# Attention and gated FFN on one core: first norm split in two, and one half of a batch's transposes issued among the output tiles

## The chip, the cores and the metric

The kernel runs on one core of a Trainium2 chip. The metric is device time in microseconds (us), the median of several executions. The engines of the core are named as in the profile: PE is TensorE's matmul, PEld its weight load, DVE is VectorE, ACT is ScalarE, POOL is GpSimd and SP is SyncE. SP, POOL and ACT also issue the DMAs. The code gives each engine its own list of instructions, in the order in which it issues them; an instruction carries the semaphore waits that it needs.

## The reference

```python
batch, n_heads, seq, head_dim = (8, 12, 448, 64)      # q, k, v: float32
n_tokens, d_model, d_ff = (3584, 768, 1536)

scores = scale * np.matmul(q, k.transpose(0, 1, 3, 2))
attn = np.maximum(scores, 0.0) ** 2 / S
x = np.matmul(attn, v)            # then [batch, seq, heads*head_dim] -> [3584, 768]

rms = np.sqrt(np.mean(x * x, axis=-1, keepdims=True) + 1e-06)
xn = x / rms * rms_g
g = xn @ w_gate
silu = g * (1.0 / (1.0 + np.exp(-g)))
val = xn @ w_val
return silu * val @ w_out
```

There are eight batches of 448 tokens. Each goes through an attention without softmax (a squared ReLU of the scores), an RMS norm over 768 features, and a gated FFN of width 1536.

## The kernel before

The order of the work is written out by hand. Matmuls of one batch's FFN (the `main` list) are interleaved by `weave` (L17) with steps of the next batch's attention (the `sides` list, each with the place in `main` before which it is issued). All operands of matmuls are bf16.

**Transposing q and k.** Scores need q and k with the head dimension on partitions. For batches 0 and 1, `pe_transposes(b, j)` (L128) does one pair of heads `j` on PE: 16 small matmuls against an identity into one PSUM tile `psT` (k in one half, q in the other), and one copy of 128x896 to the SBUF tile `qkT`, by DVE for batch 0 and by ACT for batch 1. For batches 2 and up, DMA does it: `transposes(b, half)` (L150) issues two DMA transposes on SP, `qT` (L157) and `kT` (L161), for six heads each, and `fill(b, half, gpsimd)` (L167) issues two SBUF copies on POOL (L169, L170) which bring a second copy of the transposed q to the other 64 partitions. `trans_fill` (L622) does both. `fetch(b)` (L88) loads q, k and v of a batch by three DMAs on POOL.

**Scores and values.** `pair_scores` (L194, batch 1) and `head_scores` (L213, batches 2 and up) do two matmuls into a PSUM tile `psS` (tag "psS", two buffers), then ReLU to the SBUF tile `r`, on ACT or, for some of them, on DVE. `squares` (L244) squares on DVE. `attend` (L255) multiplies with v into `psAV`, and `leave` (L279) takes it out of PSUM: `xT` (scaled by the norm's gain), and `x2`, the square for the norm, both on ACT. For batch 0's last pair `leave` squares on ACT and writes `xT` and both halves of `xD` on DVE (L294). `swap` (L302) issues two DMAs on SP which write `xD`, that is `xT` with its two halves of partitions exchanged. Matmuls of the FFN take their weight rows of one head on 64 partitions, so that gate and value run side by side on two halves of the array: six rounds use `xT` ("own", r = 0 to 5), and six use `xD` (r = 6 to 11). Two such matmuls side by side are called a pair here.

**The norm.** `norm_stat` (L401) sums `x2` by 12 matmuls with ones into `psSS`, takes the root on ACT (with a table load, and another for Silu after it), the reciprocal on DVE (`rhalf`, L424), and spreads it to `rstd` over all partitions by two copies on DVE and two on ACT (L431, L433). `norm_apply` (L436) multiplies `xT` and `xD` by `rstd` on DVE (L445), six instructions each. For batch 0 the products go to new tiles. From batch 1 on they are written over `xT`, so the product of a row must wait until the swap has read that row. For batches 2 and up the swap follows the norm.

**The stretch from batch 0's attention to its FFN** (L652 to L680). So that PE has work while batch 0's norm is not ready, three blocks of the FFN (`early_block`, PSUM tiles `psE` from a pool "mm" of four buffers) run on the raw `xT` and `xD` (`part(fb, r, ...)` does rounds r of block fb), and are scaled by `rstd` later (`early_out` copies them to SBUF on ACT, `early_scale`, `early_rest`). `units[tail:]` are the last five steps of batch 0's attention: the squares of the last pair, `leave` and `swap` of pair 4, `attend` and `leave` of pair 5. `steps` are the steps of batch 1's attention.

**The stretch from batch 0's FFN to batch 1's.** After `gate_value(0)`, six units of output tiles of batch 0 run (`out_tiles(0, 0, full)`, matmuls `psO` L399, copies `ost` L531 on ACT, stores L544 on SP). `steps[-1]`, the values, `leave` and `swap` of batch 1's last two pairs, is issued ahead of them, and `norm_stat(1)` and `norm_apply(1)` follow the first unit. Both `trans_fill(2, 0)` and `trans_fill(2, 1)` are sides of `gate_value(0)`, at 28 and 32. Then `gate_value(1)` begins, with batch 2's scores as sides: head h of batch 2 takes its `qT` and `kT` from half h // 6. Its other sides are `fetch(3)` at unit 2 and `trans_fill(3, 0)` at unit 13.

SP's order in this stretch is therefore: swaps of batch 1's pairs 0 to 3, four transposes of batch 2, the swap of batch 1's pairs 4 and 5, six stores, transposes of batch 3. POOL's is: `fetch(2)`, four fills, `fetch(3)`.

Of the kernel before, what the change touches and what calls it, by code (L numbers as in the profile page):

```python
# [8 lines left out]
FP32 = mybir.dt.float32  # L9
BF16 = mybir.dt.bfloat16  # L10
# [6 lines left out]
def weave(main, sides):  # L17

    sides = sorted(sides, key=lambda x: x[0])
    k = 0  # L20
    for n, f in enumerate(main):
        while k < len(sides) and sides[k][0] <= n:
            sides[k][1]()
            k += 1
        f()
    for _, f in sides[k:]:
        f()
# [7 lines left out]
def kernel(  # L35
# [11 lines left out]
    nc = tc.nc  # L47
    P = nc.NUM_PARTITIONS
# [79 lines left out]
    def pe_transposes(b, j):  # L128

        if b == 1 and j < 4:  # L130
            psT = ps_s.tile([P, 2, 1024], BF16, name="psT", tag="psS")
            psT = psT[:, 0, : 2 * S].rearrange("p (t s) -> p t s", t=2)
        else:
            psT = ps_m.tile([P, 2, S], BF16, name="psT", tag="mm")
        for ti, nm in enumerate(("k", "q")):
            for c in range(NCH):
                for hh in range(2):
                    nc.tensor.transpose(  # L138
                        out=psT[hh * D : (hh + 1) * D, ti, c * PC : (c + 1) * PC],
                        in_=ld[nm, b][:, 2 * j + hh, c * D : (c + 1) * D],  # L140
                        identity=ident[:],
                    )
        t = late["qkT"].tile([P, 2, S], BF16, name="qkT", tag="qkT")
        if b:
            nc.scalar.copy(out=t[:], in_=psT[:])
        else:
            nc.vector.tensor_copy(out=t[:], in_=psT[:])
        qkT[b, j] = t

# [44 lines left out]
    def pair_scores(b, j, c, on_dve):  # L194

        psS = ps_s.tile([P, 2, 512], FP32, name="psS", tag="psS")
        t = qkT[b, j]
        for hh in range(2):
            prt = slice(hh * D, (hh + 1) * D)
            flat = t[prt].rearrange("p t s -> p (t s)")  # L200
            nc.tensor.matmul(  # L201
                out=psS[:, hh, :S], lhsT=flat[:, c * PC : c * PC + P], rhs=t[prt, 1, :],
                start=True, stop=True,
            )
        if c % 2 == 0:
            raw[b, j, c] = apool.tile([PC, 2, 2, S], BF16, name="r", tag="r")
        r = raw[b, j, c - c % 2]
        if on_dve:
            nc.vector.tensor_relu(out=r[:, c % 2], in_=psS[:PC, :, :S])
        else:  # L210
            nc.scalar.activation(out=r[:, c % 2], in_=psS[:PC, :, :S], func=ACT.Relu)  # L211
# [126 lines left out]
    def attention_second(b):  # L338

        steps = []  # L340

        def visit(j, c):
            pair_scores(b, j, c, c == 3 and j > 0)
            if c == 0 and j:
                squares(b, j - 1, (2, 3))
            if c == 2:
                squares(b, j, (0, 1))

        def values(j):
            attend(b, (j, j + 1))  # L350
            leave(b, (j, j + 1))
            swap(b, j, j + 2)

        for j in range(HP):
            for c in range(NCH):
                steps.append(lambda j=j, c=c: visit(j, c))
                if c == 3 and j + 2 < HP:
                    steps.append(lambda j=j: pe_transposes(b, j + 2))
                if c == 3 and j in (2, 4):
                    steps.append(lambda j=j: values(j - 2))  # L360
                    steps.append(lambda: None)
        steps.append(lambda: squares(b, HP - 1, (2, 3)))
        steps.append(lambda: None)
        steps.append(lambda: values(HP - 2))
        return steps
# [24 lines left out]

    hTs, rstds = {}, {}

    def halves(ps, w, lhsT, rhs, start, stop):

# [4 lines left out]
    def norm_stat(b, psSS=None):  # L401


        if psSS is not None:
            psSS = psSS[:, :W]
        elif 1 < b < B - 1:
            psSS = ps_m.tile([P, S], FP32, name="psSS", tag="mm")[:, :W]
        else:
            psSS = ps_s.tile([P, 2, 512], FP32, name="psSS", tag="psS")[:, 0, :W]
        half = npool.tile([P, W], FP32, name="rhalf", tag="rhalf")  # L410
        rstd = npool.tile([P, S], FP32, name="rstd", tag="rstd")
        for kt in range(KT):
            for hf in (0, 1):
                prt = slice(HALF * hf, HALF * (hf + 1))
                nc.tensor.matmul(  # L415
                    out=psSS[prt, :], lhsT=ones_bf[:, prt],
                    rhs=x2s[b][:, kt, hf * W : (hf + 1) * W],
                    start=(kt == 0), stop=(kt == KT - 1),
                )
        nc.scalar.activation(  # L420
            out=half[:], in_=psSS, func=ACT.Sqrt, scale=1.0 / float(DM), bias=eps_col[:]
        )
        nc.scalar.activation(out=warm_act[:], in_=eps_col[:], func=ACT.Silu)
        nc.vector.reciprocal(out=half[:], in_=half[:])  # L424
        for own in (True, False):
            for hf in (0, 1):
                src = slice(HALF * hf, HALF * (hf + 1))
                dst = src if own else slice(HALF * (1 - hf), HALF * (2 - hf))
                o = rstd[dst, hf * W : (hf + 1) * W]
                if own:  # L430
                    nc.vector.tensor_copy(out=o, in_=half[src, :])  # L431
                else:
                    nc.scalar.copy(out=o, in_=half[src, :])  # L433
        rstds[b] = rstd
# [38 lines left out]
    def early_out(b, fb, parts):  # L473

        t = late["early"].tile([P, 2, S], FP32, name="gv", tag="gv")
        for part in range(2):
            nc.scalar.copy(out=t[:, part, :], in_=parts[part][:, :S])
        early[fb] = t
# [143 lines left out]
    def trans_fill(b, half):  # L622
        transposes(b, half)
        fill(b, half, nc.gpsimd)

    with tc.tile_pool(name="qkT", bufs=2, side="right") as tp, tc.tile_pool(
        name="early", bufs=EB, side="right"
    ) as ep:
        late["qkT"], late["early"] = tp, ep
        warm(12)  # L630
        steps = attention_second(1)

        def early_block(fb):
            return [ps_m.tile([P, S], FP32, name="psE", tag="mm")[:] for _ in range(2)]

        units = attention_first(0)
        tail = len(units) - 5
        for n, fn in enumerate(units[:tail]):
            fn()
            if n % 3 == 2:  # L640
                warm(2)


        raw_x = xTs[0], xDs[0]
        psSS = ps_m.tile([P, S], FP32, name="psSS", tag="mm")
        blocks = [early_block(0)]

        def part(fb, *rs):
            for r in rs:
                rounds(0, fb, blocks[fb], r, r + 1, raw_x)  # L650

        squares_last, leave_4, swap_4, attend_5, leave_5 = units[tail:]  # L652
        squares_last()
        part(0, *range(HP - 2))
        part(0, KT, KT + 1)
        leave_4()
        swap_4()
        attend_5()
        leave_5()
        part(0, KT + 2, HP - 2)  # L660
        pe_transposes(1, 0)
        norm_stat(0, psSS)
        blocks.append(early_block(1))
        part(0, HP - 1)
        part(1, *range(KT + 3))
        steps.pop(0)()
        part(0, KT + 3)
        pe_transposes(1, 1)
        steps.pop(0)()
        part(1, KT + 3)  # L670
        norm_apply(0)
        for fb in range(2):
            part(fb, KT + 4, KT + 5)
            early_out(0, fb, blocks[fb])
        for fb in range(2, EB):
            blocks.append(early_block(fb))
            for r0 in range(0, 2 * KT, KT):
                steps.pop(0)()
                rounds(0, fb, blocks[fb], r0, r0 + KT, raw_x)
            early_out(0, fb, blocks[fb])  # L680
        main = gate_value(0, EB, KT // 2)
        sides = along(6.4, 2, [lambda fb=fb: early_scale(0, fb) for fb in range(EB)])
        sides += along(10.4, 2, [lambda fb=fb: early_rest(0, fb) for fb in range(EB)])
        sides += along(0, (len(main) - 1) / len(steps), steps[:-1])
        sides += [(18.2, lambda: fetch(2))]
        sides += [(28, lambda: trans_fill(2, 0)), (32, lambda: trans_fill(2, 1))]
        weave(main, sides)
    late["ost"] = pool("ostage", 3)

# [2 lines left out]
    full = S // P  # L692
    ahead = []
    NB = 2 * FT
    weave(out_tiles(0, 0, full), [(0, steps[-1]), (1, lambda: norm_stat(1)), (1, lambda: norm_apply(1))])
    for b in range(1, B):
        main = gate_value(b)
        if b % 2:
# [46 lines left out]
```

## Time and profile before

| | us |
|---|---|
| median of 7 runs | 455.38 |
| the seven runs, sorted | 451.98, 452.86, 454.69, 455.38, 457.22, 457.36, 457.49 |
| the profiled execution | 457.35 |
| its span in the profile | 455.6 |
| PE busy | 441.6 (97%) |
| ACT busy | 285.1 (63%) |
| DVE busy | 265.0 (58%) |
| POOL busy | 53.6 (12%) |

The profiled execution took 1.75 us more than the span of its instructions. It lies at the upper end of the seven runs. All positions below are us from the start of the span. In the 20 us from 60 to 80, PE was busy for 20.00 and in those from 80 to 100 for 16.17, at a mean granted clock of 1.00 and 0.83. A PE matmul of 64x448 has a duration of 0.35 us at the full clock, and in a steady stream one pair follows another after 0.19 us. Ends of matmuls are modelled in the profile, so short gaps on PE can be missing from its list of waits.

### The profile page before, as it was taken

Reading aid. Unit: us, or ns where it says so; the run is one execution under the profiler, and the core shown is the slowest. Engines: PE = TensorE matmul, PEld = TensorE weight load, DVE = VectorE, ACT = ScalarE, POOL = GpSimd, SP = SyncE. Lnnn points to the kernel's source line nnn. Section 1 sums busy time; section 2 is a strip of 40 time slices with the busy share of each in tenths; the row PEclk is TensorE's granted clock in tenths of the full one; section 3 lists DMA queues with packets and bytes.
Section 4 is the critical chain, followed back from the end, with each engine's and each line's share of the span. In section 5 each row is a group of like instructions: output and inputs, shape, how many; then the busy total and the mean of one; then the engine's idle time right before and its main releaser. Section 6 shows DMA issues by size and latency. Waiting matters only on the chain.

```text
span 455.6 us, 10951 instructions
## 1 busy us (share of the span) xinstructions
PE 441.6 (97%) x4768; PEld 248.3 (55%) x4768; DVE 265.0 (58%) x341; ACT 285.1 (63%) x434; POOL 53.6 (12%) x79
## 2 busy tenths in 40 slices
PE   7998999889999999999999999999999999999996
PEld 3434555545556555655556555655556555565564
DVE  4979975368655566466754566476754366542210
ACT  4899886547766677566757577566757667552221
POOL 8343300400000300002000300003000000000000
PEclk9999999979999999999999999999999999999999
DMA  9999999995104995079913998069922900041013
GB/s 136 198 202 201 202 213 176 173 247 89 32 1 113 194 187 74 1 166 181 155 32 83 196 194 94 1 124 190 165 53 56 217 21 1 1 117 51 1 36 106
DMA packets 86832, 53.32 MB, mean 117 GB/s; under 512 B 36608, under 2 KB 80896, under 8 KB 86784
## 3 DMA queue, kind: packets, MB, share of 16 engines
q0 software_dynamic: 44496, 27.50, 42.1%
q1 hardware_dynamic: 41664, 24.56, 27.7%
q8 instruction: 37, 0.61, 0.6%
q10 hardware_dynamic: 624, 0.57, 0.4%
q14 instruction: 11, 0.09, 0.1%
HBM read 47.19 MB, written 11.01 MB: 128 GB/s over the span
## 4 chain that ended last, share of the span: by engine, by line
PE 91%; ACT 4%; DVE 2%; DMA 2%; issue 1%; ACTq 0%; SPq 0%; DVEq 0%
PE psG L465 39%; PE psO L399 22%; PE psAV L267 9%; PE psV L465 8%; PE psS L222 7%; PE psW L605 2%; DMA xD<-xT 2%; PE psS L181 1%; ACT r L191 1%; PE psT L138 1%; PE psS L201 1%; PE psE L465 1%; PE psSS L415 1%; DVE rhalf L424 1%; ACT ost L531 1%
## 5 line engine op out<-in xcount | busy, mean ns | idle before, releaser
L465 PEld LDWEIGHTS <-wgv_sb 64*128 64x128 bf16 x2304 | 122.3, 95 | 102.4 <-issue 16.7
L465 PE MATMUL psG<-xT,wgv_sb 64*128 64x448 bf16 x558 | 123.5, 352 | 3.8 <-DVE xT L445 3.8
L465 PE MATMUL psV<-xT,wgv_sb 64*128 64x448 bf16 x558 | 123.3, 353 | 0.0
L465 PE MATMUL psV<-xD,wgv_sb 64*128 64x448 bf16 x558 | 122.2, 351 | 0.0
L465 PE MATMUL psG<-xD,wgv_sb 64*128 64x448 bf16 x558 | 122.2, 351 | 0.0
L236 ACT ACTIVATE r<-psS 112x896 bf16<-112x896 f32 x108 | 96.1, 917 | 28.5 <-PE psS L222 28.4
L399 PE MATMUL psO<-wo_sb,hT 128*64 128x512 bf16 (+2 forms) x1368 | 113.7, 323 | 0.0
L511 DVE TENSOR_TENSOR hT<-sil,psV 128x448 bf16<-128x448 bf16 x93 | 57.6, 620 | 96.3 <-ACT sil L509 95.1
L399 PEld LDWEIGHTS <-hT 128*64 128x64 bf16 x1368 | 73.9, 110 | 36.1 <-issue 4.1
L509 ACT ACTIVATE sil<-psG 128x448 bf16<-128x448 f32 x93 | 50.7, 545 | 59.3 <-PE psV L465 41.9
L240 DVE TENSOR_TENSOR r<-r 112x1792 bf16<-112x1792 bf16 x72 | 78.4, 1089 | 11.1 <-ACT r L236 10.1
L531 ACT COPY ost<-psO 128x512 f32<-128x512 f32 (+2 forms) x57 | 26.2, 472 | 42.4 <-PE psO L399 35.8
L222 PE MATMUL psS<-qT,kT 64*128 64x448 bf16 (+1 forms) x288 | 47.4, 354 | 0.4 <-DVE r L234 0.4
L299 ACT ACTIVATE xT<-psAV,ga_sb 128x448 bf16<-128x448 f32 x47 | 27.5, 631 | 24.7 <-PE psAV L267 24.7
L234 DVE TENSOR_SCALAR r<-psS 112x896 bf16<-112x896 f32 x36 | 39.1, 1086 | 5.8 <-PE psS L222 5.8
L267 PE MATMUL psAV<-r,vb 112*64 112x448 bf16 x384 | 41.5, 356 | 0.0
L169 POOL DMA_DIRECT2D qT<-qT x12 | 6.5, 540 | 273.7 <-DMA qT<-qb 200.1
L424 DVE RECIPROCAL rhalf<-rhalf 128x224 f32<-128x224 f32 x8 | 12.4, 1554 | 38.0 <-ACT rhalf L420 38.0
L445 DVE TENSOR_TENSOR xT<-xT,rstd 128x448 bf16<-128x448 bf16 x48 | 26.5, 621 | 8.5 <-DMA xD<-xT 6.7
L267 PEld LDWEIGHTS <-vb 112*64 112x64 bf16 x384 | 19.4, 109 | 20.1 <-issue 8.7
L222 PEld LDWEIGHTS <-kT 64*128 64x128 bf16 (+1 forms) x288 | 16.9, 97 | 19.8 <-issue 8.7
L250 DVE TENSOR_TENSOR r<-r 112x1792 bf16<-112x1792 bf16 x23 | 24.5, 1086 | 1.8 <-ACT r L211 1.8
(57 smaller groups left out, 257.5 us busy)
## 6 DMA issues: line engine op xcount, KB each, us to landing
vb<-in_v_dram POOLq DMA_DIRECT2D x7, 672.0 KB, 18.5
qb<-in_q_dram POOLq DMA_DIRECT2D x6, 672.0 KB, 12.4
kb<-in_k_dram POOLq DMA_DIRECT2D x6, 672.0 KB, 15.3
qT<-qT POOLq DMA_DIRECT2D x24, 168.0 KB, 4.5
xD<-xT SPq DMA_DIRECT2D x24, 168.0 KB, 3.0
out_dram<-ost SPq DMA_DIRECT2D x7, 336.0 KB, 5.6
wgv_sb<-in_moe_w_gate_dram POOLq DMA_DIRECT2D x6, 384.0 KB, 16.8
wgv_sb<-in_moe_w_val_dram POOLq DMA_DIRECT2D x6, 384.0 KB, 16.9
```

Source lines behind the costliest of these rows:

```text
L222: nc.tensor.matmul(out=psS[: end - o, hf, :S], lhsT=flat[prt, o:end], rhs=qT[prt, 1 - hf : 3 - hf, h % HH], start=True, stop=True,)
L234: nc.vector.tensor_relu(out=r[:, cp], in_=src)
L236: nc.scalar.activation(out=r[:, cp], in_=src, func=ACT.Relu)
L240: nc.vector.tensor_tensor(out=r[:], in0=r[:], in1=r[:], op=ALU.mult)
L267: nc.tensor.matmul(out=part[hh * D : (hh + 1) * D, :], lhsT=ld["v", b][:, 2 * j + hh, c * D : (c + 1) * D], rhs=rsq[b, 2 * j + hh, c], sta ...
L299: nc.scalar.mul(out=xTs[b][:, j, :], in_=psAV[:, i, :], mul=ga_sb[:, j : j + 1])
L399: nc.tensor.matmul(out=ps[prt, :w], lhsT=lhsT[:, prt], rhs=rhs, start=start, stop=stop)
L445: nc.vector.tensor_tensor(out=x[:, kt, :], in0=raw_x[:, kt, :], in1=rstds[b][:], op=ALU.mult)
L465: nc.tensor.matmul(out=parts[part][:, :S], lhsT=wgv_sb[prt, h, fb * P : (fb + 1) * P], rhs=src[prt, kt, :], start=(r == 0), stop=(r == 2 * ...
L509: nc.scalar.activation(out=s[:], in_=psG, func=ACT.Silu)
L511: nc.vector.tensor_tensor(out=hT[:, fb, o : o + S], in0=s[:], in1=psV, op=ALU.mult)
L531: nc.scalar.copy(out=osts[i, t][:, o : o + w], in_=ps[:, :w])
```

## The change

1. `pe_transposes`: for batch 0's first pair, `psT` is two PSUM tiles instead of one, and each is copied on its own (two DVE copies of 128x448 in place of one of 128x896), the k half while q is still to come. For batch 1's first pair the copy moves from ACT to DVE.
2. `attention_second`: the ReLU of pair 1's last chunk moves from DVE to ACT (the fourth chunk of a pair is on DVE from pair 2 on, not from pair 1).
3. `norm_stat` ends after the reciprocal. The spread to `rstd` is a function of its own, `norm_spread`, called at once for all batches but 0. For batch 0, one visit of batch 1's scores (matmuls, and a ReLU on ACT) is written between the two.
4. The order of the parts after batch 0's attention is new: two own rounds of block 0 and batch 1's first transposes come ahead of `leave_4`, `swap_4`, `attend_5`, and more rounds come behind. Batch 1's second transposes move behind the first `early_out`.
5. `trans_fill(2, 1)` moves from `gate_value(0)` (side at 32) to the output tiles (side at 2). SP's order becomes: two transposes of batch 2, the swap of batch 1's pairs 4 and 5, the two stores of tile 0, the two other transposes of batch 2, four stores. POOL's order stays.

The number of instructions of each engine stays but for one more copy on DVE and what moves between DVE and ACT by 1 and 2.

```diff
+            parts = [psT[:, 0], psT[:, 1]]
+        elif b == j == 0:
+            parts = [ps_m.tile([P, S], BF16, name="psT", tag="mm")[:] for _ in range(2)]
         else:
             psT = ps_m.tile([P, 2, S], BF16, name="psT", tag="mm")
-        for ti, nm in enumerate(("k", "q")):
+            parts = [psT[:, 0], psT[:, 1]]
+        t = late["qkT"].tile([P, 2, S], BF16, name="qkT", tag="qkT")
+        for ti, (nm, part) in enumerate(zip(("k", "q"), parts)):
...
-        t = late["qkT"].tile([P, 2, S], BF16, name="qkT", tag="qkT")
-        if b:
+            if b == j == 0:
+                nc.vector.tensor_copy(out=t[:, ti, :], in_=part)
+        if b and j:
             nc.scalar.copy(out=t[:], in_=psT[:])
-        else:
+        elif b or j:
             nc.vector.tensor_copy(out=t[:], in_=psT[:])
...
-            pair_scores(b, j, c, c == 3 and j > 0)
+            pair_scores(b, j, c, c == 3 and j > 1)
...
         nc.vector.reciprocal(out=half[:], in_=half[:])
+        halfs[b] = half
+        if b:
+            norm_spread(b)
+
+    def norm_spread(b):
+
+        half = halfs.pop(b)
+        rstd = npool.tile([P, S], FP32, name="rstd", tag="rstd")
         for own in (True, False):
...
         squares_last()
-        part(0, *range(HP - 2))
-        part(0, KT, KT + 1)
+        part(0, 0, 1)
+        pe_transposes(1, 0)
         leave_4()
         swap_4()
         attend_5()
         leave_5()
-        part(0, KT + 2, HP - 2)
-        pe_transposes(1, 0)
+        part(0, 2, 3, KT, HP - 2)
         norm_stat(0, psSS)
         blocks.append(early_block(1))
+        part(0, KT + 1, KT + 2)
+        part(1, *range(KT))
         part(0, HP - 1)
-        part(1, *range(KT + 3))
         steps.pop(0)()
+        norm_spread(0)
+        part(1, *range(KT, KT + 3))
         part(0, KT + 3)
-        pe_transposes(1, 1)
         steps.pop(0)()
         part(1, KT + 3)
         norm_apply(0)
         for fb in range(2):
             part(fb, KT + 4, KT + 5)
             early_out(0, fb, blocks[fb])
+            if fb == 0:
+                pe_transposes(1, 1)
...
-        sides += [(28, lambda: trans_fill(2, 0)), (32, lambda: trans_fill(2, 1))]
+        sides += [(28, lambda: trans_fill(2, 0))]
...
-    weave(out_tiles(0, 0, full), [(0, steps[-1]), (1, lambda: norm_stat(1)), (1, lambda: norm_apply(1))])
+    weave(out_tiles(0, 0, full), [(2, lambda: trans_fill(2, 1)), (0, steps[-1]), (1, lambda: norm_stat(1)), (1, lambda: norm_apply(1))])
```

More of the change, by code (lines that the diff above doesn't have):

```diff
@@ L138, in pe_transposes @@
                     nc.tensor.transpose(
-                        out=psT[hh * D : (hh + 1) * D, ti, c * PC : (c + 1) * PC],
+                        out=part[hh * D : (hh + 1) * D, c * PC : (c + 1) * PC],
                         in_=ld[nm, b][:, 2 * j + hh, c * D : (c + 1) * D],
@@ L389, in attention @@
         return steps
-    hTs, rstds = {}, {}
+    hTs, rstds, halfs = {}, {}, {}
     def halves(ps, w, lhsT, rhs, start, stop):
@@ L410, in norm_stat @@
         half = npool.tile([P, W], FP32, name="rhalf", tag="rhalf")
-        rstd = npool.tile([P, S], FP32, name="rstd", tag="rstd")
         for kt in range(KT):
```

## The prediction

> **What bounds the kernel now.** I read the page first. PE is busy 97% of the span, so time can come only from PE's gaps or from its clock. The strip over 40 slices of 11.4 us shows one place with both:
>
> ```profile
> PE   7998999889999999999999999999999999999996
> ...
> PEclk9999999979999999999999999999999999999999
> ```
>
> The clock strip has a single 7, slice 8 (91 to 102 us). PE's share is below 9 in slices 0, 3, 7, 8 and the last. PE's list of waits over the whole span then gives the sizes:
>
> ```profile
> PE psG L465 <- DVE xT L445: 3.8, 1, 3.8
> PE psS L181 <- ACT r L191: 1.5, 3, 0.8
> PE psS L201 <- ACT r L211: 1.2, 2, 0.9
> ```
>
> One wait is larger than all others: gate_value(1) waits for a product of batch 1's norm. The stretches of 2 us around it show gap and clock (PE's busy time is the first pair of columns; PEclk is the third number from the end):
>
> ```profile
> 88.00:90.00 2.00, 1.32 (x18) 0.59 (x13) 0.00 (x0) 0.37 (x1) 0.00 (x0) 1.00 1.00 207
> 90.00:92.00 2.00, 0.00 (x0) 0.00 (x0) 0.00 (x0) 0.00 (x0) 0.00 (x0) 0.95 1.29 214
> 92.00:94.00 2.00, 0.84 (x4) 0.31 (x5) 1.52 (x3) 0.00 (x0) 0.00 (x0) 0.50 1.19 325
> 98.00:100.00 2.00, 2.00 (x20) 1.11 (x18) 0.22 (x1) 0.98 (x3) 0.00 (x0) 0.84 1.46 199
> ```
>
> Who holds it up is told by the chain of waits, and by SP's timeline:
>
> ```profile
> 84.31 0.48 SPq L305
> 84.83 7.55 DMA xD<-xT
> 92.47 0.64 DVE xT L445
> 93.16 0.53 PE psG L465
> ```
> ```profile
> 70.00 2.37 SPq L157 DMA_TRANSPOSE qT<-qb  x1
> 74.89 2.36 SPq L161 DMA_TRANSPOSE kT<-kb  x1
> 77.29 4.20 SPq L157 DMA_TRANSPOSE qT<-qb  x1
> 81.53 1.44 SPq L161 DMA_TRANSPOSE kT<-kb  x1
> 83.08 2.37 SPq L305 DMA_DIRECT2D xD<-xT  x2
> ```
>
> The swap of batch 1's last two pairs could go at 77.4 (ACT has written both rows of xT by 77.39), but SP is issuing the second half of batch 2's transposes until 82.97. The swap goes at 83.08, lands at 92.4, and DVE may write xT rows 4 and 5 only then.
>
> **Part 5, the transposes behind the output tiles.** In the new SP order the swap follows the first kT transpose, whose issue ends at 77.25. Two swap DMAs took 1.1 us of SP at 68.5 and 2.4 us at 83, so they are issued by 79.8. Their landing took 5.4 us at 68 and 7.5 to 8.9 us at 83. So the swap lands between 83 (77.4 + 5.4) and 88 (79 + 8.9). `rstd` is ready at 83.6 and the first four products of xT take 2.23 us as before; the last two end between 87 (swap by 85.8) and 89.1 (swap at 88). PE leaves the output tiles at 88.39 and needs row 4 after four pairs, at 88.39 + 4 x 0.19 = 89.15. No gap is left at the early end; at the late end row 4 is there at 88.6. The xD products (six, 3.3 us) end between 90.3 and 92.4; their first use is behind two blocks of own rounds, at about 91. The late end costs PE some 0.4 us there. I take none: 85.8 lies beyond the sum by the 5.4 us row.
>
> What that is worth: before, the two score matmuls at 98.95 are reached after 4 pairs (88.39 to 89.15) and 16 more slots (14 pairs, two of scores), which at 0.19 take 3.04 us. They would be at 92.19 instead of 98.95, a gain of 6.76 us. Of it 4.0 are the gap (89.15 to 93.16) and 2.75 the half clock from 93.16 to about 98.5.
>
> The Trainium skill ("TensorE: Matmul & The Clock Gate", Part 1) says that the gate halves the clock after an idle window of about 3.4 us and gives it back after one busy window of that length, the window running freely. By that rule the restart would cost half of 3.4, 1.7 us, and the gain would be 5.7; the trace has 5.3 us at half clock, and I go by the trace. By the same rule an idle time of 4 us need not hold a whole window, so runs without the drop are possible; no run here shows it.
>
> What the moved transposes meet: on SP they stand behind the two stores of tile 0, which wait for ACT's second ost copy (ends 83.85). Two stores at 0.9 us each (six took 5.48), so qT is issued at 85.7, for 2.4 to 4.2 us, and kT by 90. Behind them wait four stores; their ost tiles are not reused before the output tiles at 130, so nothing waits for that. qT lands 3.6 to 11.3 us after its issue (rows of this kernel: 3.6, 6.3, 11.3); at 6.3 it is 92. On POOL the two fills of this half wait for it, and `fetch(3)` is queued behind them: it starts at about 93.4 instead of 85.1. Its q and k took 13.5 and 16.1 us to land, so they are there at 107 to 111; batch 3's transposes went at 108.7 before, and batch 3's first scores were at 144.2 (137.4 with the gain). The fills land after 2.6 to 7.3 us, so the second half is ready by 97 to 100. Its first score (head 6) was at 112.54 and moves to 105.8. Cover is 6 us or more; with the longest row of each it is 85.7 + 11.3 + 1.2 + 1.1 + 7.3 = 106.6, a gap of 0.8.
>
> Against the move speaks a rule of the skill ("Trainium Kernel Development and Optimization", Key Constraints): DMAs of all queues share the same 16 engines and interleave. By it an earlier place in a queue need not mean an earlier landing, since the loads of vb and the first transposes are in flight; that is the late end above, 88, and still takes no more than 0.4 us from the sum.
>
> **Parts 2 to 4, batch 0's norm.** Here PE, ACT and DVE are all nearly full, and the chain alternates:
>
> ```profile
> 34.64 1.56 DVE rhalf L424
> 36.23 0.38 ACT rstd L433
> 36.99 0.81 ACT r L211
> 37.80 0.79 ACT qkT L145
> 38.59 0.81 ACT r L211
> 39.41 0.85 ACT gv L477 x2
> ```
>
> PE's listed gaps from 33 to 40 are 0.29 (for ACT's rhalf), 0.86 (for ACT's r) and 0.32 (for ACT's gv), together 1.47 us; that is the upper bound of the gain. In the new order PE gets to `attend_5` with two fewer pairs (0.37) ahead of it, ACT's rhalf no longer stands behind the qkT copy (0.8), and the reciprocal starts about 0.3 earlier (behind DVE's xT and xD of the last pair, which wait for ACT's square). The first ReLU fills ACT's wait for the reciprocal (0.52). I count PE's slots: it comes to `part(0, 10)`, the first use of pair 4's xD, at about 36.2 instead of 38.23. But swap_4 is issued behind the same ACT work as before, at 31.30 and 31.80, and its two DMAs take 6.1 and 6.6 us: they land at 37.4 and 38.4. So a new wait of some 2 us takes the place of the 0.86, and from there both orders go on from 38.4. In the new one ACT's ReLU is already done, and its gv copies start near 38.9 instead of 39.41, but the qkT copy of pair 1 is still to do (0.8). Beyond, ACT has the same amount of work (one copy less, one ReLU more), DVE 0.4 less (0.62 added, 1.08 removed), and both are full until ACT's idle 1.18 at 54.5. I take a gain of 0.3; the bounds are -0.8 (the copy that is now late, uncompensated) and +1.47.
>
> **Part 1.** The first DVE copy (0.62, at 6.76) becomes two of about 0.35; the first can run while q is transposed, and the scores at 7.44 come 0.27 earlier at best. DVE is full from 9.0 to 20, so the lead is kept until the loads bind. I take 0.2, bounds 0 and 0.3.
>
> **Sum.** 6.76 + 0.3 + 0.2 = 7.3 us off the profiled execution: 457.35 - 7.3 = 450.1. This execution is 2.0 us above the median of the seven, and three of the seven lie at 457.2 to 457.5. The lowest is 5.4 below it, which is less than the loss at 89 to 98. I read that as this gap being of different length in different runs; then the runs after lie near 450, not at 455.38 - 7.3 = 448.1. I take 449.7, a little below the first.
>
> **Rivals.**
>
> *A next wait takes part of it.* At 89.5 PE wants batch 2's first scores, before 94.0. They need the fills of the first half, issued at 81.87 and landing 6.2 us later, 88.1 to 88.6. Cover is only about 1 us. For it speaks that margin; against it, that these fills shared the engines with the second half's transposes, which now come later. If they land in 11.3 (the longest transpose row), PE waits 4 us at 93, perhaps with the half clock: the gain falls to 3.5 or less, time 453.5. 0.11.
>
> *The second half comes too late (slower).* If qT and kT of the second half each meet the longest landing, one behind the other, the chain above grows by another 11.3 to 117.9: PE waits 12.1 us at 105.8, then 2.75 for the clock, so 457.35 - 7.3 + 14.9 = 465. It turns slower when the fills land after 112, 5.5 us later than the sum of the longest rows. Nothing in the rows shows that. 0.05.
>
> *The swap lands no sooner.* If it waits for the loads of vb and the first transposes until 92, only the second half's issue is gone and the time stays within 2 us of now: 455. What speaks against it is the swap at 68, which landed in 5.4 us in full DMA traffic. 0.06.
>
> *Batch 0's stretch loses its lower bound*, -0.8, with nothing else wrong: 451.1 to 451.5, in the forecast's range. The forecast: 0.78.
>
> **How the numbers follow.** Within 1%, 4.55 us, no change can be told from a measurement of this kernel: the border is 450.8. The forecast's own range is 447.5 (all from the median, or all the stretch's gaps) to 451.6. About 0.09 of its 0.78 lie above 450.8. Faster is 0.69 + 0.01 of the first rival; same is 0.09 + 0.10 + 0.06; slower 0.05. Eight in ten takes the forecast's range and the nearer part of the first rival: 447.4 to 453.
>
> **What would show it.** Right: no wait of psG on xT, clock strip without the 7, SP's xD issue near 77.4 and its landing before 88, four stores behind the transposes, fetch(3) near 93. A wait of psE on the DMA xD near 36 to 38 shows swap_4. Wrong: a wait of psS on qT or kT near 89 or 106, or PE idle past 3 us anywhere.

## The result, and the profile after

The changed kernel takes 449.75 us (median of 12 runs, 448.92 to 451.87); the kernel before takes 454.95 (31 runs, 451.35 to 460.4). The ratio is 0.9894, with a 95% interval of 0.9867 to 0.9922. The profiled execution after took 449.78 against 457.35 before, its span 447.9 against 455.6. Ratios leave out runs more than 1.5% above the fastest of their kernel, medians do not; this matters below for e5, whose ratio rests on three of its six runs, and for e3, where 4 of the 23 runs beside it are left out.

The page's strips of the kernel after, PE's busy tenths and the granted clock:

```profile
PE   7998999999999999999999999999999999999996
...
PEclk9999999999999999999999999999999999999999
```

The 7 in the clock strip is gone, and PE's slices 7 and 8 are at 9. The first two rows of PE's list of waits over the whole span (total, times, longest):

```profile
PE psS L187 <- ACT r L197: 1.5, 3, 0.8
PE psE L478 <- DMA xD<-xT: 1.3, 2, 0.7
```

The wait of psG on xT is not in it. The second line is new, in batch 0's stretch. SP's timeline of the kernel after (start, duration, instructions), and then POOL's:

```profile
74.50 3.06 SPq L167 DMA_TRANSPOSE kT<-kb  x1
77.60 1.26 SPq L311 DMA_DIRECT2D xD<-xT  x2
82.89 0.84 SPq L557 DMA_DIRECT2D out_dram<-ost  x2
83.78 2.97 SPq L163 DMA_TRANSPOSE qT<-qb  x1
86.79 1.71 SPq L167 DMA_TRANSPOSE kT<-kb  x1
88.60 2.51 SPq L557 DMA_DIRECT2D out_dram<-ost  x4
```
```profile
89.89 0.53 POOL L175 DMA_DIRECT2D qT<-qT  x1 [6.85 <-DMA qT<-qb]
90.40 0.53 POOL L176 DMA_DIRECT2D qT<-qT  x1
90.91 0.99 POOL L95 DMA_DIRECT2D qb<-in_q_dram  x1
```

The swap is issued at 77.60, right behind the first kT transpose; the second half follows the stores of tile 0, and `fetch(3)` follows its fills. DVE then runs all twelve products without a break:

```profile
82.63 3.30 DVE L458 TENSOR_TENSOR xT<-xT,rstd 128x448 bf16<-128x448 bf16 x6 [0.24 <-ACT rstd L446]
85.85 3.30 DVE L458 TENSOR_TENSOR xD<-xD,rstd 128x448 bf16<-128x448 bf16 x6
```

Where the time went is read from PE's own starts in the two timelines:

| start on PE, us | before | after | lead |
|---|---|---|---|
| first scores of batch 0 | 7.44 | 6.88 | 0.56 |
| first early round (psE) | 29.71 | 29.14 | 0.57 |
| first block of gate_value(0) (psG) | 43.36 | 42.21 | 1.15 |
| values of batch 1's pairs 4 and 5 (psAV) | 74.48 | 73.53 | 0.95 |
| first block of gate_value(1) (psG) | 88.39 | 87.44 | 0.95 |
| batch 2's first values (psAV) | 109.76 | 102.04 | 7.72 |
| end of the span | 455.6 | 447.9 | 7.7 |

From 88 to 110 the lead grows by 6.77; all the rest of the change is in the 0.95 before it, and nothing is won or lost after 110. These are the two profiled executions, and the one before is a long one: between the medians the change is worth 5.2 us.

### The profile page after: what moved, and what is told of

Same layout as the page of the kernel before. It is cut to its first block, busy times and chain, and to the rows that moved or that the text cites. A ratio compares the mean times of both kernels' runs of the same rounds, so it can differ in the third digit from the quotient of the medians.

```text
span 447.9 us, 10949 instructions
## 1 busy us (share of the span) xinstructions
PE 438.0 (98%) x4768; PEld 246.8 (55%) x4768; DVE 264.5 (59%) x342; ACT 284.7 (64%) x434; POOL 53.7 (12%) x79
## 4 chain that ended last, share of the span: by engine, by line
PE 90%; ACT 6%; DMA 1%; DVE 1%; issue 1%; ACTq 0%; SPq 0%; DVEq 0%
PE psG L478 38%; PE psO L405 24%; PE psAV L273 8%; PE psV L478 8%; PE psS L228 7%; PE psW L618 2%; ACT r L217 2%; DMA xD<-xT 1%; ACT r L197 1%; PE psS L187 1%; PE psSS L420 1%; ACT gv L490 1%; ACT qkT L151 1%; PE psT L143 1%; PE psS L207 1%
## 5 line engine op out<-in xcount | busy, mean ns | idle before, releaser
L478 PEld LDWEIGHTS <-wgv_sb 64*128 64x128 bf16 x2304 | 120.9, 94 | 97.1 <-issue 10.3
L478 PE MATMUL psG<-xT,wgv_sb 64*128 64x448 bf16 x558 | 121.8, 349 | 0.0
L478 PE MATMUL psV<-xT,wgv_sb 64*128 64x448 bf16 x558 | 121.4, 349 | 0.1
```

The costliest lines, as they stand in the source:

```text
L478: nc.tensor.matmul(out=parts[part][:, :S], lhsT=wgv_sb[prt, h, fb * P : (fb + 1) * P], rhs=src[prt, kt, :], start=(r == 0), stop=(r == 2 * ...
```

## The experiments

From the values of pairs 4 and 5 to batch 2's first values PE takes 35.28 us before and 28.51 after. That length, less 28.51, is the loss at the gap; it is used for the profiles below.

**e1, the kernel before once more,** no edit.

> The kernel before, unchanged, to see how its runs differ. Theory (the gap of PE ahead of batch 1's FFN is of different length in different runs): median 454 to 456, runs spread over 451 to 458, and the lower the mean granted clock of a run the longer it takes; the profile shows the wait of psG on xT again, somewhere between 1 and 4 us, ending at a swap that SP issues only at 83. Rival (the spread is noise from elsewhere): times and clocks of the runs do not go together, and the gap in this profile is again 3.8 us whatever the time.

Median 455.45, 451.88 to 457.21. The four runs at a mean clock of 0.998 to 1.000 took 451.88 to 452.78; the eight at 0.990 to 0.996 took 454.38 to 457.21. So in these runs clock and time go together. In the runs of the same kernel beside the other experiments the two groups meet: those at 0.998 or more took 450.88 to 454.50, those at 0.996 or less 453.96 and more. The profile (455.37) has a shorter gap and a shorter half clock; first the row of PE's waits, then its stretches of 2 us, with PEclk third from the end:

```profile
PE psG L465 <- DVE xT L445: 2.9, 1, 2.9
```
```profile
92.00:94.00 2.00, 1.77 (x10) 0.81 (x11) 2.00 (x5) 0.26 (x1) 0.00 (x0) 0.56 1.26 169
94.00:96.00 2.00, 2.00 (x16) 0.91 (x13) 1.93 (x4) 0.66 (x1) 0.00 (x0) 0.59 1.22 284
96.00:98.00 2.00, 2.00 (x26) 1.12 (x22) 0.16 (x1) 1.65 (x3) 0.00 (x0) 1.00 1.24 291
```

The loss at the gap is 4.79 here, against 6.77 in the first profile. The gap's length and the half clock differ between these two executions, as the theory had it. No profile of this kernel at full clock was taken, so the gap of those runs was not seen.

**e2, the move alone.**

```diff
-        sides += [(28, lambda: trans_fill(2, 0)), (32, lambda: trans_fill(2, 1))]
+        sides += [(28, lambda: trans_fill(2, 0))]
...
-    weave(out_tiles(0, 0, full), [(0, steps[-1]), (1, lambda: norm_stat(1)), (1, lambda: norm_apply(1))])
+    weave(out_tiles(0, 0, full), [(2, lambda: trans_fill(2, 1)), (0, steps[-1]), (1, lambda: norm_stat(1)), (1, lambda: norm_apply(1))])
```

> The kernel before with only the second half of batch 2's transposes moved to the output tiles. Theory (nearly all of the gain is this move): median 450.7, that is 1.0 above the whole change (449.75), span 448.8 (455.6 less 6.76), no wait of psG on xT, no 7 in the clock strip, spread of the runs as narrow as after the change (3 us). Rival (the gain comes from batch 0's stretch and the split copy): 454 or more.

Median 450.06 (449.80 to 450.87), ratio 0.9899 (0.9866 to 0.9932); span 448.1, no wait of psG, loss at the gap 0.00. The move alone brings nearly all. It came out better than the 450.7 expected; in its profile the first scores started at 6.73 without the split copy (see point 3 below).

**e3, all but the move** (the kernel after, with those two lines put back).

> The whole change without that move (the transposes stay in gate_value(0)). Theory: median 454.0, that is 0.95 below the kernel before, the wait of psG on xT and the half clock still there, runs spread over 6 us. Rival (batch 0's stretch brings the gain): 450 or less, no gap.

Median 454.76 beside 455.30 for the kernel before on that chip; ratio 1.0022 (0.9992 to 1.0053). The gain of 0.95 expected from the rest is not seen: the ratio shows none, and the medians, 0.54 apart with runs spread over 6 us, can't tell 0.95 from nothing. PE's waits, SP's swap and DVE's late products of this kernel:

```profile
PE psG L478 <- DVE xT L458: 3.6, 1, 3.6
```
```profile
84.00 2.25 SPq L311 DMA_DIRECT2D xD<-xT  x2
```
```profile
91.19 1.16 DVE L458 TENSOR_TENSOR xT<-xT,rstd 128x448 bf16<-128x448 bf16 x2 [6.40 <-DMA xD<-xT]
```

PE reaches gate_value(1) at 87.37, 1.02 before the kernel before, but the swap is issued when it was (84.00 against 83.08): SP's transposes are timed by the loads of q and k, not by PE: from 60 to 110 SP's list of waits has 10.7 us for q's and 1.7 for k's load here, 8.0 and 2.5 before. So the lead of the other parts ends in a wait, as this profile shows it. With the move in they count by what e2 and the whole change differ in, ratios of 0.9899 and 0.9894, which these runs can't tell from nothing.

**e4, batch 1's second transposes in the wait for swap_4.** An attempt to do better than the change.

```diff
         part(1, KT + 3)
+        pe_transposes(1, 1)
         norm_apply(0)
...
-            if fb == 0:
-                pe_transposes(1, 1)
```

> The whole change, with batch 1's second transposes moved back ahead of the rounds that wait for swap_4, so that PE's 0.43 us of transposes and ACT's 0.8 us copy fall into their waits there (1.35 us on PE, 0.68 on ACT). Theory (after swap_4 lands ACT is the bound of this stretch): gate_value(0) starts 0.4 to 0.7 earlier, at 41.5 to 41.8 instead of 42.21, and the median is 449.2. Rival (PE gives the lead back before 60, where it waits for ACT's ReLU anyway): 449.75, no change.

Median 449.72 against 449.75, ratio 0.9889 against 0.9894: no change. From the first early round to gate_value(0) PE takes 12.92 us instead of 13.07, 0.15 less and not 0.4 to 0.7. ACT's timeline shows its idle 0.68 filled by the copy, but the gv copies then stand behind it, and PE waits for them:

```profile
36.71 0.91 ACT L217 ACTIVATE r<-psS 112x896 bf16<-112x896 f32 x1
37.52 0.89 ACT L151 COPY qkT<-psT 128x896 bf16<-128x896 bf16 x1
38.30 1.81 ACT L490 COPY gv<-psE 128x448 f32<-128x448 f32 x4
```
```profile
PE psE L478 <- ACT gv L490: 0.4, 1, 0.4
```

**e5 and e9, the kernel before with that one swap on ACT's queue.** All four transposes stay where they were.

```diff
-            swap(b, j, j + 2)
+            swap(b, j, j + 2, nc.scalar if j == HP - 2 else None)
```

> The kernel before, with only the swap of batch 1's last two pairs issued by ACT instead of SP; all four transposes of batch 2 stay ahead of the output tiles and are in flight with it. Theory (the swap was late because of its place behind the transposes in SP's queue): it is issued near 78.3, lands by 88, no wait of psG on xT over 0.5 us, clock strip without the 7; ACT loses about 1 us for the issue, off PE's path; median 450.7, as with the move alone. Rival (it is late because the transposes keep the DMA engines busy, whatever the queue): it lands after 90, the gap stays over 1 us, and the median is 453 or more.

The median of the six runs is 454.02; the ratio, of the three lower ones, is 0.9899 (0.9844 to 0.9954). The SP and ACT queues in the profile (of a lower run), and DVE's products:

```profile
77.42 3.04 SPq L157 DMA_TRANSPOSE qT<-qb  x1
80.50 3.15 SPq L161 DMA_TRANSPOSE kT<-kb  x1
```
```profile
77.29 1.18 ACTq L305 DMA_DIRECT2D xD<-xT  x2
```
```profile
83.46 3.30 DVE L445 TENSOR_TENSOR xT<-xT,rstd 128x448 bf16<-128x448 bf16 x6 [0.24 <-ACT rstd L433]
```

The swap is issued at 77.29, with the second half's transposes in flight beside it, its two DMAs land 5.0 and 6.5 us after their issue, and DVE no longer stops. So the place in SP's queue was the cause, not the load on the DMA engines. Three of the six runs took 450.22 to 450.58, but three took 457.45 to 458.74, at a mean clock of 0.991 and none with a profile, so the kernel was run again:

> The kernel before with only the swap of batch 1's last two pairs issued by ACT, once more: three of its six runs took 450.2 to 450.6 at full clock, three 457.5 to 458.7 at a mean clock of 0.991. Theory (beside the transposes the swap, or the fills behind them, still land late in some executions, and PE then stands idle long enough to lose the clock): runs fall into the same two groups, 450.4 and 458; a profile of the upper group would show a wait of psG on xT or of psS on qT. Rival (a disturbance of those runs): all runs near 450.4.

Ten runs on another chip: median 450.31 (449.99 to 452.57), ratio 0.9912 (0.9877 to 0.9946), none at 457. What the three were stays open: no trace of them was kept, so a late swap in some executions is not excluded.

**e6, dummy matmuls in the gap.** 18 matmuls of 128x448 on a constant tile, in the kernel before; their result is not used.

```diff
...
-        sides = []
+        sides = [(0, lambda: warm_s(18))] if b == 1 else []
```

> The kernel before, with 18 more matmuls of 128x448 on a constant tile (3.4 us, their result is not used) just ahead of batch 1's first FFN block, where PE else stands idle. Theory (the loss is the gap and, in most runs, the half clock after it): the gap's end stays where the swap lands, near 92, but the clock is not halved after it; mean clock 0.999 or more in all runs; median 452.6, like the three runs of the kernel before at full clock (451.9 to 452.8). Rival (the clock costs nothing of its own, or falls for another reason): median 455.4 or more.

Median 454.07 (453.35 to 459.05, eleven of twelve at 455.35 or less), ratio 0.9984 (0.9955 to 1.0012). PE's timeline, and the stretch that had no matmul before:

```profile
87.96 3.58 PE L611 MATMUL psW<-warm_in 128*128 128x448 bf16 x18
91.47 0.36 PE L465 MATMUL psG<-xT,wgv_sb 64*128 64x448 bf16 x1
```
```profile
90.00:92.00 2.00, 2.00 (x15) 0.90 (x14) 0.95 (x2) 0.00 (x0) 0.00 (x0) 1.00 0.96 143
```

The clock stays up (0.998 or more in eleven of twelve runs, 0.996 in one), and the loss at the gap is 3.91: it is the dummies' own 3.51 and 0.4 behind them, where PE waits for a product of xD, no longer gap and half clock. That the clock can be held is shown. That it is worth 2.8 in the median, as expected, is not. A likely reason, which no profile shows, is that in some executions the gap is shorter than the dummies.

**e7, the second half later, behind fetch(3) on POOL.** How much cover has the move?

```diff
-    weave(out_tiles(0, 0, full), [(2, lambda: trans_fill(2, 1)), (0, steps[-1]), (1, lambda: norm_stat(1)), (1, lambda: norm_apply(1))])
+    weave(out_tiles(0, 0, full), [(0, steps[-1]), (1, lambda: norm_stat(1)), (1, lambda: norm_apply(1))])
...
             sides += [(2, lambda b=b: fetch(b + 2))]
+            if b == 1:
+                sides += [(6, lambda: trans_fill(2, 1))]
```

> The whole change, with the second half of batch 2's transposes at unit 6 of gate_value(1): on SP behind all six stores, on POOL its fills behind fetch(3), so that they share the DMA engines with it. This measures how much cover the moved half has: its first scores (head 6) stand at about 104.8 in the trace after. Theory: qT is issued near 90.5, lands at 97 to 102, the fills land at 104 to 109, so PE waits 0 to 4 us for psS of head 6; median 450 to 454. Rival (the cover is wide even so): no wait, 449.75. Rival (slower than before): a wait of over 5 us and half clock, 457 or more.

Median 461.71 (four runs, 459.91 to 463.96), slower than the kernel before: ratio 1.0158 (1.0095 to 1.0221). The rival on the slow side came true. SP's and POOL's timelines, the chain of waits and PE's stretches of 4 us:

```profile
88.59 4.52 SPq L163 DMA_TRANSPOSE qT<-qb  x1
93.16 5.44 SPq L167 DMA_TRANSPOSE kT<-kb  x1
```
```profile
82.73 0.99 POOL L95 DMA_DIRECT2D qb<-in_q_dram  x1
...
102.32 0.56 POOL L175 DMA_DIRECT2D qT<-qT  x1 [16.71 <-DMA qT<-qb]
```
```profile
93.16 16.64 DMA kT<-kb
109.81 3.34 issue
113.14 1.01 PE psS L228 x2
```
```profile
108.00:112.00 4.00, 0.00 (x0) 0.00 (x0) 0.00 (x0) 0.00 (x0) 0.00 (x0) 0.51 1.17 97
```

The transposes land 13.1 and 16.6 us after their issue, not 6 to 11, and PE stands before head 6's scores from 104.7 to 113.14. The landing of kT at 109.81 is not what ended that wait: 3.34 us more pass, for which the chain names nothing. POOL's fills, issued at 102.32 and landing 10.7 us later, at 113.0, fit it; the same fills took 5.4 us in the kernel after. So both the transposes and the fills behind them were late.

**e8, as late on SP, but ahead of fetch(3) on POOL.**

```diff
-    weave(out_tiles(0, 0, full), [(2, lambda: trans_fill(2, 1)), (0, steps[-1]), (1, lambda: norm_stat(1)), (1, lambda: norm_apply(1))])
+    weave(out_tiles(0, 0, full), [(0, steps[-1]), (1, lambda: norm_stat(1)), (1, lambda: norm_apply(1))])
...
+            if b == 1:
+                sides += [(2, lambda: trans_fill(2, 1))]
             sides += [(2, lambda b=b: fetch(b + 2))]
```

> The whole change, with the second half of batch 2's transposes at unit 2 of gate_value(1), ahead of fetch(3): on SP behind all six stores, as in the run with unit 6, but on POOL its fills stand ahead of fetch(3), as in the change. Theory (that run lost its time because batch 3's loads went ahead on POOL and shared the DMA engines with the transposes, not because SP issued them 5 us later): qT is issued near 88.6 and lands in about 6 us, the fills go near 95 and land by 102, PE does not wait for head 6 at 104, median 449.75. Rival (the place on SP is what makes it late): PE waits for head 6, median 455 or more.

Median 449.54 (five runs, 449.18 to 451.94), ratio 0.9880 (0.9798 to 0.9962), no wait for head 6. SP and POOL in its profile (451.94, the longest of the five; its starts lie some 2.4 us later from batch 0's stretch on, for which see point 2 below):

```profile
91.09 1.52 SPq L163 DMA_TRANSPOSE qT<-qb  x1
92.66 1.97 SPq L167 DMA_TRANSPOSE kT<-kb  x1
```
```profile
95.66 0.52 POOL L175 DMA_DIRECT2D qT<-qT  x1 [12.59 <-DMA qT<-qb]
96.17 0.52 POOL L176 DMA_DIRECT2D qT<-qT  x1
96.68 0.97 POOL L95 DMA_DIRECT2D qb<-in_q_dram  x1
```

Now they land in 4.0 and 4.1 us. The half could go 5 us later on SP at no cost; what made e7 slow was that batch 3's loads went first.

## Why the prediction was right, point by point

1. **The gap, 6.76 us.** Measured 6.77 between the two profiles. The swap was issued at 77.60 (said: 77.4), its two DMAs landed 5.3 and 5.6 us after their issue, by 83.9 (said: 83 to 88), so the sharing of the DMA engines that the prediction set against the move cost nothing here. Rows 4 and 5 followed the first four products at once, and the scores that had been at 98.95 were at 91.24, 6.76 earlier than 98.95 less the lead of 0.95. e2 has this term alone, e5 and e9 show that its cause is the place in SP's queue.

2. **Batch 0's stretch, 0.3.** From the first early round to gate_value(1) it is 58.68 before and 58.30 after, 0.38. The new wait for swap_4 is there, 1.35 us in the list where 2 were said. The chain of waits of the kernel after, in order of time:

```profile
31.23 6.30 DMA xD<-xT
37.54 0.04 issue
37.58 0.38 PE psE L478 x2
```

It has the place that the reciprocal had in this chain before. The 0.58 won up to gate_value(0) goes back to 0.38 by 74. It is not always so: in e4's profile the same length is 58.07, 0.23 less than in the kernel after, and a gain of that size can't be told from nothing in the medians.

What the prediction left out here is the clock. The bound of -0.8 for this stretch counted only work, but the new wait for swap_4 can bring the half clock too. In e8, which has the same order here, it did:

```profile
PE psE L478 <- DMA xD<-xT: 2.1, 2, 1.4
```
```profile
38.00:40.00 2.00, 1.64 (x21) 0.97 (x22) 2.00 (x5) 1.15 (x3) 0.57 (x2) 0.72 1.46 200
40.00:42.00 2.00, 2.00 (x14) 0.84 (x12) 2.00 (x5) 2.00 (x4) 0.66 (x2) 0.50 1.46 194
```

From the first early round to gate_value(1) that execution takes 60.53, 1.85 more than the kernel before. In the kernel after the two waits were 0.69 and 0.66 us, not 1.38 and 0.67, and the clock stayed at 1.00. Two of its twelve runs, 451.32 and 451.87 at a mean clock of 0.994 and 0.995, may be of e8's kind; no profile shows them.

3. **The split copy, 0.2.** The lead at the first scores is 0.56, but most of it is how the two profiled executions started. From the first transpose to the first scores, the profiles in which q's transposes start 0.37 behind k's take 1.69, 1.74 and 1.55 us without the split (before, e1, e5) and 1.39 and 1.44 with it (e3, e4); those with 0.22 take 1.36, 1.37 and 1.37 without (e2, e6, e9) and 1.23 and 1.23 with it (after, e7); e8, with 0.45 behind, takes 1.33. So the split is worth 0.1 to 0.3, as said, and the rest is the start, which falls into the one case or the other whatever the kernel.

4. **The sum was added as if its terms were independent.** They are not: without the move, the lead of the other two ended in the wait at the gap in e3's profile, and no gain was seen. The total held because the move is in.

5. **From the profiled execution to the median.** The step that took 450.1 from the profile and not 448.1 from the median was right: after the change the profile (449.78) lies at the median, and the profiled kind was the long one of the seven runs shown. That the gap and the half clock spread the runs before is supported, not shown run by run: e1's two groups differ in clock, its profile has a shorter gap, and with the clock held (e6) eleven of twelve runs lie within 2 us. That the median came within 0.05 us of the 449.7 is luck: the last step, "a little below the first", was not worked out, and in the 449.78 there is the lead of 0.56 at the start, of which 0.3 to 0.5 is chance (point 3).

6. **What the moved transposes meet.** qT was issued at 83.78 (said: 85.7), its fills at 89.89 (92 to 93), `fetch(3)` at 90.91 (93.4), batch 3's transposes at 103.16 and 106.54 (107 to 111); head 6's first scores ran at 104.82 without a wait. The fills of the first half landed 3.2 us after 81.87 and were needed at 88.59; that rival had about 3 us of cover where 1 was given.

7. **Where the working was wrong: the bound on the late side.** The prediction took 11.3 us, the longest landing of a transpose in the trace, as the end of the range, and said that nothing in the rows shows more. e7 had 13.1 and 16.6 beside batch 3's loads, fills of 10.7 where it had taken 7.3 at most, and a median 6.4 us above that of the kernel before beside it (455.35). The change is safe because POOL's order holds those loads back behind the fills, a wait that the prediction had counted only as a possible cost.

## What to carry to other kernels

Look first at which instruction stands ahead of the late DMA in its own issuing queue: moving two transposes behind one swap, or the swap to another queue, was worth some 5 us of 455 in the medians and 7 against the long profiled execution, while the hand-tuning of a full stretch showed no gain as long as a later wait, timed by loads, took it back. A gap on PE cost its length and, in the profiles here in which it was 2.9 us or more, the half clock after it, so a wait whose length differs from run to run also spreads the runs. A new wait of the same kind, put in for a small gain, can bring it too (point 2). When a transfer is moved later, ask what bulk loads it will then share the engines with; a wait that holds those loads back can be what makes the move work.

## What the runs showed of the hardware

The half clock came in pieces of one length. Twice the missing share of the clock, summed over the stretches, is the time at half clock: 3.4 us in e1 (0.44 and 0.41 of 2 us), 3.4 in e3 (0.13, 0.50 and 0.22), 3.4 in e8 (0.28, 0.50 and 0.07), 6.8 in the kernel before (0.05, three times 0.50 and 0.16), 10.2 in e7 (0.48, four times 0.50 and 0.08). The waits ahead of it were 2.9, 3.6, 2.05 (1.38 and 0.67 with one matmul between), 3.8 and 8.4 us. That is one, one, one, two and three times 3.4 us, the window that the Trainium skill gives ("TensorE: Matmul & The Clock Gate", Part 1). But the page lets the clock fall after an idle window of that length, and in e1 and e8 it fell behind waits of 2.9 and 2.05 us; for this kernel the measurement decides. In the kernel before it was not back after one window: 5.3 us of the 6.8 lay behind the restart, where the prediction's estimate by that page was 3.4. That the same kernel runs at a mean clock of 0.998 or more and at 0.996 or less, which the page's freely running window allows, is what e1 showed.

DMA transposes of the same shape landed 4.0 us after their issue with the loads held back (e8) and 13.1 to 16.6 beside them (e7), and SP was held by the issue of one for 1.5 and 2.0 us in the first case and for 4.5 and 5.4 in the second.
